# One weight sum per step, and the experts' fifth tile transposed one row tile later

## The chip, the cores and the metric

The kernel runs on one core of a Trainium2 chip. Its time is the device time of one execution in microseconds (us). The engines of the core are named as in the profile: PE is TensorE (PEld its weight load), DVE is VectorE, ACT is ScalarE, POOL is GpSimd, and SP is SyncE, which here does nothing but issue DMA transfers.

## The reference

Three stages follow each other: a linear attention with an exponential feature map, a layer that takes the largest of three products, and a mixture of 8 experts in which each token goes to its two best.

```python
def phi(x):                                   # attention, 4 x 8 heads, 576 tokens, 64 wide
    proj = np.einsum('bhsd,df->bhsf', x, w_phi)
    proj = proj - np.max(np.abs(proj), axis=-1, keepdims=True)
    return np.concatenate([np.exp(proj), np.exp(-proj)], axis=-1)
...
num = np.einsum('bhsf,bhfd->bhsd', q_p, kv)
den = np.einsum('bhsf,bhf->bhs', q_p, z)[..., None] + 1e-06
...
h = np.maximum(np.maximum(x @ w1, x @ w2), x @ w3)      # x: 2304 x 512, w: 512 x 768
x = h @ w_out
...
noisy_logits = x @ w_gate + np.log1p(np.exp(x @ w_noise)) * noise
top2 = np.argpartition(-noisy_logits, 2, axis=1)[:, :2] # softmax over the two gives top2_w
for e in range(8):
    for k in range(2):
        mask = top2[:, k] == e
        h = np.maximum(x[mask] @ w1[e], 0.0)            # w1[e]: 512 x 1024, w2[e]: 1024 x 512
        out[mask] += top2_w[mask, k, None] * (h @ w2[e])
```

## The kernel before

The program is a list of steps, each with a planned time. `at` puts a step at a time, `pe` puts one at the running PE clock and moves that clock on, and `after` puts one at a distance from it. The steps are then issued in the order of their planned times, so a planned time sets only the place in the queue of each engine. PE, ACT, DVE and SP take their instructions in just that order. On POOL a scheduler decides.

Every float32 product is done as three products of shortened numbers: a weight or an activation is split into a high part (an ACT copy) and a low part (a DVE subtraction), as in `split`, and high x high, high x low and low x high are added up in PSUM.

The second stage works on 6 chunks `c` of 384 tokens. For each of 6 column blocks `f` of 128 hidden units it makes three products (`first`, L886, 12 instructions each, `j` = 0, 1, 2), takes their maximum (`larger`: ACT copies the first into a tile `a`, L894, and DVE takes the larger twice, L896), splits it (`hidden`, tiles `hh` and `hl`) and multiplies by the output weights (`second`, L913, 9 instructions), one step later. The product banks `s` are three and are used in turn, so the ACT copy of one step must be done before PE can begin a later one. At the end of a chunk its output goes to memory (`x2_out`), is transposed (L927) and routed; the routing's result is scattered into a table by six indirect DMAs on POOL (L1047). In chunk 0 the last of the weights arrive in 64-bit form and are made narrow on the way: POOL adds two parts (`narrow_add`, L243), DVE masks (L262) and ACT and DVE split them.

The experts 1 to 7 use a seven-product scheme for their first layer, which needs sums and differences of quarters of their weights. These are made during the second stage, 28 of them (7 experts, 4 each). One such sum is: two loads on SP into a buffer `raw` (`quarter_load`), four POOL additions (`quarter_sum`), an ACT copy into the tile `qh`, of which there is one (`quarter_high`), and a DVE subtraction and two stores to the table `sums` on SP (`quarter_out`). There are two buffers with the tag `raw` and one `raw3`; every third sum takes `raw3`. `sum_jobs` plans them: the load 9.5 ahead of the end of a step `f`, the additions 4.5 ahead, the copy and the stores 0.65 behind. One sum stands in each `f` of chunks 1 to 4 but two at `f` = 4 in chunks 1, 2 and 3, and one in chunk 5. In chunk 5 the weights of expert 0 are loaded too (`refill`, `w2_load`).

The experts' part goes over units of up to 608 tokens: 28 `product` steps of 6 instructions each (L1183), then five row tiles of the second layer (`expert2`, L1324, 24 instructions a row tile). Between the row tiles stand the transposes of the next expert's tokens (`turns7`, `turn_x`, L1119), which POOL has gathered (L1109), two tiles ahead; `rows7` then forms the sums and splits of those tokens on ACT and DVE (L1147, L1158, L132). The fifth tile has 96 tokens and is transposed behind row tile 3 (`i == 2`).

Of the kernel before, what the change touches and what calls it, by code (L numbers as in the profile page):

```python
# [9 lines left out]
F32 = mybir.dt.float32  # L10
# [9 lines left out]
P = 128  # L20
# [3 lines left out]
class Plan:  # L24
# [5 lines left out]
    def at(self, t, f, *x):  # L30
        self.ops.append((t, len(self.ops), f, x))
# [7 lines left out]
def tile_linear_attention__then__moe__then__noisy_top2_moe(  # L39
# [28 lines left out]
    F1 = FF1 // P  # L68
# [23 lines left out]
    st, pools = {}, {}  # L92
# [59 lines left out]
    def raw_tile():  # L152
        return stage.tile([P, 1024], F32, name="raw", tag="raw", bufs=2)
# [915 lines left out]
    def sizes(M):  # L1069
        return [min(P, M - i * P) for i in range((M + P - 1) // P)]  # L1070
# [267 lines left out]
    def summed(key, i):  # L1338
        return isinstance(key, int) and key >= SEVEN and i < len(ORDER7) and SEVENTHS[ORDER7[i]][0] == "S"

    def w2_load(key, e, i):
        if summed(key, i):
            return
        raw = raw_tile()
        first_ = len(ORDER7) if isinstance(key, int) and key >= SEVEN else KD
        if i >= first_:
            f = i - first_
            dq.dma_start(raw.rearrange("p (a d) -> p a d", a=2),
                         e_w2[ds(e, 1), f * 2 * P:(f + 1) * 2 * P, :].rearrange("o (a p) d -> p (o a) d", p=P))
        elif first_ == KD:  # L1350
            dq.dma_start(raw, e_w1[ds(e, 1), i * P:(i + 1) * P, :].rearrange("o p f -> p (o f)"))
        else:
            i_, j_ = SEVENTHS[ORDER7[i]][1]
            dq.dma_start(raw.rearrange("p (a f) -> p a f", a=2),
                         e_w1[e, j_ * 2 * P:(j_ + 1) * 2 * P, i_ * (FF2 // 2):(i_ + 1) * (FF2 // 2)]
                         .rearrange("(a p) f -> p a f", p=P))
        st["w2", key, i] = raw
# [148 lines left out]
    def pe(dur, f, *x):  # L1506
        at(clock[0], f, *x)
        clock[0] += dur

    def after(d, f, *x):  # L1510
        at(clock[0] + d, f, *x)

    def first_pe(c, f, j):
        pe(G1, first, c, f, j)
        after(0.05, larger, j)
        if j == 2:
            after(0.6, hidden, c, f)
# [33 lines left out]
    for i, n in enumerate(late_ones[1:]):  # L1551
        t = END + 5.0 + 2.6 * i + 3.0 * (i > 5)
# [7 lines left out]
    def finish(c):  # L1560

        for t in range(CT):
            after(0.05 + 0.5 * t, x2_out, c, t)

    def tail(c, i):
        if i == 0:
            for t in range(2):
                pe(0.45, x2_turn, c, t)
                after(0.0, x2_in, c, t)
            if c < NCHUNK - 1:  # L1570
                after(0.1, begin_route, c)
        elif i == 1:
            pe(0.45, x2_turn, c, 2)
            after(0.0, x2_in, c, 2)
        elif i == 2:
            pe(0.95, gates, c)
            after(0.0, gates_out, c)
        else:
            pe(0.35, gates_turn, c)
            route_at(c, clock[0])  # L1580
# [7 lines left out]
    def base(e):  # L1588
        return 12 + pairs.index((e, 0))
# [10 lines left out]
    def refill(i, n, wait=0.1):  # L1600
        for i in range(i, i + n):
            if i >= len(pairs):
                return
            after(0.0, w2_room, *pairs[i], i + 12)
            if summed(*pairs[i]):
                after(wait + 1.0 + 3.0 * (i % 4), w2_high, *pairs[i])
                continue
            en, j = pairs[i]
            t = max(clock[0] + wait, split_at[-1] + 3.0)
            at(max(split_at[-2] + 0.01, t - 9.0), w2_load, en, en, j)  # L1610
            at(t, w2_high, en, j)
            at(t, w2_low, en, j)
            split_at.append(t)

    def refill_at(i, t, lead):
        if i < len(pairs):
            en, j = pairs[i]
            t += clock[0]
            at(max(split_at[-2] + 1.21, t - lead), w2_load, en, en, j)
            at(t, w2_high, en, j)  # L1620
            at(t + 1.2, w2_low, en, j)
            split_at.append(t)
# [6 lines left out]
    jobs = [(e, a, c) for e in range(SEVEN, E) for a in range(2) for c in range(2)]  # L1629
    todo = list(jobs)  # L1630

    def sum_jobs(n):
        for i, job in enumerate(todo[:n]):
            after(-9.5, quarter_load, *job)
            after(-4.5 + i, quarter_sum, *job)
            after(0.65 + 0.02 * i, quarter_high, *job)
            after(0.66 + 0.02 * i, quarter_out, *job)
        del todo[:n]

    for c in range(NCHUNK):  # L1640
        if c == NCHUNK - 1:
            split_at.append(clock[0] + 25.0)
        for f in range(F1):
            for j in range(3):
                if c or f or j > 1:
                    first_pe(c, f, j)
                if c and j == 2:
                    sum_jobs(2 if f == 4 and c < 4 else 1)
                if c and f == 0 and j == 0:
                    pe(G2, second, c - 1, F1 - 1)  # L1650
                    finish(c - 1)

                tails = TAILS[c == NCHUNK - 1]
                if c and 3 * f + j in tails:
                    tail(c - 1, tails.index(3 * f + j))
            fx = 3 if c else 4
            if f in (fx, fx + 1) and c + 1 < NCHUNK:
                after(0.5, split_x, c + 1, f - fx)
            if c == NCHUNK - 1 and f == F1 - 1:
                break  # L1660
            if f:
                pe(G2, second, c, f - 1)
            if c == NCHUNK - 1 and f % 2 == 1:
                refill(2 * f - 2, 3)
            if c == NCHUNK - 1 and f and f % 2 == 0:
                refill(2 * f - 1, 1)
    c = NCHUNK - 1
# [27 lines left out]
    for n, (e, M, row0) in enumerate(units):  # L1695
# [77 lines left out]
        def turns7(i, n=n):  # L1773
            pe(0.45, turn_x, n + 1, cap, i)
            if i + 2 < len(sizes(cap)):
                after(0.02, gather_x, n + 1, cap, i + 2, N + 1)

        def rows7(j, wait=1.6):
            after(0.5, x_quarters, j)
            after(wait, x_sums, j)  # L1780

        if M <= P:
            pe(0.7 * 2, expert2, n, e, M, 0, range(2))
            pe(0.45, tile_turn, n, 1)
            after(0.0, tile_hidden, n, 1)
            turns7(4)
            rows7(2)
            pe(0.7 * 2, expert2, n, e, M, 0, range(2, 4))
            pe(d2 / 2, expert2, n, e, M, 0, range(4, F2))
            after(0.0, expert_out, n, e, M, 0)  # L1790
        else:
            if nxt and n > 0:
                for i in range(2):
                    turns7(i)
                rows7(0)
            if not nxt:
                after(0.9, settle)
            for i in range(len(sizes(M))):
                if n == 0 and i == 2:
                    pe(0.45, turn_x, 1, cap_b, 0)  # L1800
                    after(0.02, gather_x, 2, cap, 1, N + 1)
                    turns7(0, 1)
                if n == 0 and i == 3:
                    turns7(1, 1)
                    rows7(0)
                pe(d2, expert2, n, e, M, i)
                if n == 0:
                    after((-0.01, -0.01, 0.5, 0.0)[i], expert_out, n, e, M, i)
                else:
                    after(0.95 if nxt and i == 1 else -0.01, expert_out, n, e, M, i)  # L1810
                if n == 0 and i == 2:
                    after(0.51, gather_prev, n, e, M, 3)
                elif n and i + 3 < len(sizes(M)):
                    after(0.96 if nxt and i == 1 else 0.0, gather_prev, n, e, M, i + 3)
                if nxt and n > 1:
                    if i == 1:
                        turns7(2)
                        turns7(3)
                        rows7(1)
                    if i == 2:  # L1820
                        turns7(4)
                        rows7(2)
        if n == 0:
# [3 lines left out]
        if n:  # L1827
            if seven(n):
                i = base(e) + len(ORDER7)
# [3 lines left out]
            else:  # L1833
                i = base(e) + 2
# [61 lines left out]
```

## Time and profile before

| | us |
|---|---|
| median of 3 runs | 947.41 |
| lowest, highest | 946.42, 951.82 |
| profiled execution | 951.02 |
| its span | 949.3 |
| PE busy in the span | 930.8 (98%) |
| PE's weight load busy | 808.1 (85%) |
| DVE, ACT, POOL busy | 609.2, 491.8, 539.4 |

Times within the profile are counted from the start of its span. A row of the timeline is one instruction or a few alike in sequence, with start, duration, engine, line and what it writes and reads; the bracket at its end is the time for which its engine had been idle and what ended that. A matmul's duration overlaps the next one's, so the distance of two starts is what one costs.

### The profile page before, as it was taken

How to read it: one execution, taken by the hardware profiler on the slowest of the kernel's cores; microseconds unless marked ns; L12 is line 12 of the kernel's file. 1: busy time of each engine (PE TensorE's matmuls, PEld its weight loads, DVE VectorE, ACT ScalarE, POOL GpSimd, SP SyncE). 2: the span in 40 equal slices, each digit the busy share in tenths (PEclk: the TensorE clock that was granted, in tenths of full speed). 3: DMA queues.
4: the chain of work that ended last, by engine and by line, in shares of the span. 5: the costliest groups of instructions: out<-in, count | busy, mean ns of one | idle time of the engine just before them, and what ended most of it. 6: DMA issues, size and time to landing. Idle time of an engine off the chain costs nothing. (4 is left out here: it accounts for less than half of the span.)

```text
span 949.3 us, 18471 instructions
## 1 busy us (share of the span) xinstructions
PE 930.8 (98%) x6817; PEld 808.1 (85%) x6817; DVE 609.2 (64%) x1292; ACT 491.8 (52%) x1056; POOL 539.4 (57%) x598
## 2 busy tenths in 40 slices
PE   8999999999999999899999999999999999999997
PEld 7777777889989989799997889798898979799895
DVE  6999998895644546355445357757675767657641
ACT  6999998464333244342335246545363645545340
POOL 6888898454464735456153546555574746546362
PEclk9999999999999999999999999999999999999999
DMA  7666653541567676656446266857575746648312
GB/s 201 174 208 176 187 169 117 197 134 56 187 203 243 181 244 208 196 191 189 157 159 219 68 206 218 292 183 259 168 250 182 279 160 208 238 160 303 96 34 72
DMA packets 129372, 174.91 MB, mean 184 GB/s; under 512 B 35806, under 2 KB 90206, under 8 KB 129282
## 3 DMA queue, kind: packets, MB, share of 16 engines
q1 hardware_dynamic: 117794, 143.79, 47.7%
q0 software_dynamic: 10928, 29.62, 9.3%
q8 instruction: 54, 0.88, 0.4%
q10 hardware_dynamic: 560, 0.33, 0.1%
q14 instruction: 36, 0.29, 0.1%
HBM read 123.05 MB, written 51.24 MB: 184 GB/s over the span
## 5 line engine op out<-in xcount | busy, mean ns | idle before, releaser
L886 PE MATMUL s<-xh,wh 128*128 128x384 f32 x432 | 149.0, 345 | 5.1 <-ACT a L894 4.2
L886 PE MATMUL s<-xh,wl 128*128 128x384 f32 x432 | 146.0, 338 | 0.4 <-DVE wl L278 0.4
L886 PE MATMUL s<-xl,wh 128*128 128x384 f32 x432 | 145.9, 338 | 0.0
L1334 POOL DMA_INDIRECT out_dram<-o,emeta x40 | 49.0, 1224 | 103.0 <-DVE o L1332 51.0
L886 PEld LDWEIGHTS s<-xh,wh 128*128 128x128 f32 x432 | 81.6, 189 | 12.5 <-ACT a L894 5.5
L896 DVE TENSOR_TENSOR a<-s,a 128x384 f32<-128x384 f32 x72 | 39.9, 555 | 72.2 <-PE s L886 71.0
L1324 PE MATMUL p<-wh,hh 128*128 128x512 f32 (+1 forms) x208 | 82.9, 399 | 0.0
L886 PEld LDWEIGHTS s<-xl,wh 128*128 128x128 f32 x432 | 81.7, 189 | 1.4
L1324 PE MATMUL p<-wh,hl 128*128 128x512 f32 (+1 forms) x208 | 82.4, 396 | 0.1
L886 PEld LDWEIGHTS s<-xh,wl 128*128 128x128 f32 x432 | 81.7, 189 | 0.7 <-DVE wl L278 0.7
L1324 PE MATMUL p<-wl,hh 128*128 128x512 f32 (+1 forms) x208 | 82.1, 395 | 0.0
L1409 DVE TENSOR_TENSOR wl<-raw,wh 128x1024 fp32r<-128x1024 f32 x57 | 69.1, 1218 | 14.8 <-ACT wh L1401 14.7
L1183 PE MATMUL s<-gx,wh 128*128 128x304 f32 x336 | 72.5, 302 | 0.0
L1377 POOL TENSOR_TENSOR raw<-raw 128x256 f32<-128x256 f32 x28 | 24.3, 866 | 83.3 <-DMA raw<-in_moe_w_dram 39.8
L1401 ACT ACTIVATE wh<-raw 128x1024 fp32r<-128x1024 f32 x57 | 58.9, 1054 | 24.1 <-PE p L1324 11.2
L1047 POOL DMA_INDIRECT meta<-mt,si x36 | 37.4, 1040 | 48.3 <-DVE si L1043 39.1
L132 DVE TENSOR_TENSOR gx<-t,gx 128x512 fp32r<-128x512 f32 (+3 forms) x88 | 41.0, 481 | 34.3 <-ACT gx L131 34.0
L243 POOL TENSOR_TENSOR nm<-nm,bits 128x512 int32<-128x512 int32 (+1 forms) x32 | 38.2, 1204 | 42.5 <-DVE nm L233 26.6
L1391 DVE TENSOR_TENSOR raw<-raw,qh 128x1024 fp32r<-128x1024 f32 x28 | 37.0, 1320 | 35.6 <-ACT qh L1386 35.6
L131 ACT ACTIVATE hh<-a 128x384 fp32r<-128x384 f32 x36 | 18.8, 522 | 74.4 <-DVE a L896 74.4
L1183 PEld LDWEIGHTS s<-gx,wh 128*128 128x128 f32 x336 | 55.6, 189 | 0.7
L131 ACT ACTIVATE gx<-t 128x512 fp32r<-128x512 f32 (+3 forms) x88 | 36.4, 436 | 38.1 <-DVE t L1158 29.9
(316 smaller groups left out, 2645.4 us busy)
## 6 DMA issues: line engine op xcount, KB each, us to landing
raw<-in_moe_w_dram SPq DMA_DIRECT2D x57, 512.0 KB, 4.5
raw<-in_moe_w_dram SPq DMA_DIRECT2D x56, 256.0 KB, 4.3
sums<-qh SPq DMA_DIRECT2D x28, 512.0 KB, 3.0
sums<-raw SPq DMA_DIRECT2D x28, 512.0 KB, 3.6
wh<-sums SPq DMA_DIRECT2D x28, 512.0 KB, 4.9
wl<-sums SPq DMA_DIRECT2D x28, 512.0 KB, 6.3
bits<-in_moe_w_dram SPq DMA_DIRECT2D x18, 512.0 KB, 5.5
out_dram<-zrow SPq DMA_DIRECT2D x9, 512.0 KB, 4.0
```

The costliest lines, as they stand in the source:

```text
L131: nc.scalar.activation(hi, src, AF.Copy)
L132: nc.vector.tensor_tensor(lo, src, hi.bitcast(F32), op=ALU.subtract)
L243: in_order(nc.gpsimd.tensor_tensor(m_[:, i:i + w], m_[:, i:i + w], low[:, i:i + w], op=ALU.add))
L886: nc.tensor.matmul(p_, a[:, d, fs], b_, start=(n == 0), stop=(n == 3 * KD - 1))
L896: nc.vector.tensor_tensor(a, p_, st.pop("a"), op=ALU.max)
L1047: ins = nc.gpsimd.indirect_dma_start(out=meta, out_offset=bass.IndirectOffsetOnAxis(ap=si[:, t, kk:kk + 1], axis=0), in_=mt[:, t, kk, :], ...
L1183: nc.tensor.matmul(bk["p"], a[:, d, fs], b_[:, d, :], start=(d == 0 and i == 0), stop=(d == 1 and i == 2))
L1324: nc.tensor.matmul(p_, a, b_[:, fw], start=(f == 0 and r == 0), stop=(f == (3 if seven(n) else F2 - 1) and r == 2))
L1334: alone(e, nc.gpsimd.indirect_dma_start(out=out, out_offset=bass.IndirectOffsetOnAxis(ap=mt[:m, i, 1:2], axis=0), in_=o[:m], in_offset=Non ...
L1391: nc.vector.tensor_tensor(lo, t, hi.bitcast(F32), op=ALU.subtract)
L1401: nc.scalar.activation(WE[e, i][0], st["w2", e, i], AF.Copy)
L1409: nc.vector.tensor_tensor(wl, st.pop(("w2", e, i)), wh.bitcast(F32), op=ALU.subtract)
```

## The change

Three things are changed. `sum_jobs` becomes `sum_job`, which plans one sum per call; the loads are planned 15.5 ahead of the step's end and the additions 10.5 ahead. It is called at `j` = 2 of every `f` in chunks 1 to 5 and at the last `f` of chunk 0, so that the first sum falls into chunk 0, and three into chunk 5. At `f` = 3 and 4 the copy and the stores are planned at 1.8 behind the step's end. In the first refill (expert 0) the second, fifth and eighth load take the buffer `raw3`. In the experts the transposes of the fifth tile, and the sums and splits behind them, are planned behind row tile 4 (`i == 3`).

```diff
     def w2_load(key, e, i):
         if summed(key, i):
             return
-        raw = raw_tile()
+        if key == 0 and i % 3 == 1 and "m2" in pools:
+            raw = pools["m2"].tile([P, 1024], F32, name="raw3", tag="raw3")
+        else:
+            raw = raw_tile()
...
-    def sum_jobs(n):
-        for i, job in enumerate(todo[:n]):
-            after(-9.5, quarter_load, *job)
-            after(-4.5 + i, quarter_sum, *job)
-            after(0.65 + 0.02 * i, quarter_high, *job)
-            after(0.66 + 0.02 * i, quarter_out, *job)
-        del todo[:n]
+    def sum_job(t, ahead=15.5):
+        if todo:
+            job = todo.pop(0)
+            after(-ahead, quarter_load, *job)
+            after(5.0 - ahead, quarter_sum, *job)
+            after(t, quarter_high, *job)
+            after(t + 0.01, quarter_out, *job)
...
-                if c and j == 2:
-                    sum_jobs(2 if f == 4 and c < 4 else 1)
+                if j == 2 and (c or f == F1 - 1):
+                    sum_job(1.8 if f in (3, 4) else 0.65)
...
-                    if i == 2:
+                    if i == 3:
                         turns7(4)
                         rows7(2)
```

On ACT, at `f` = 4 of chunk 3 (`a` frees PE's bank, `xh` and `hh` are splits, `qh` is the copy of a weight sum), before:

```order
L894 ACTIVATE a_5345<-s_5315 128x384
L131 ACTIVATE xh<-xT 128x768
L131 ACTIVATE hh<-a_5378 128x384
L1386 ACTIVATE qh<-raw 128x1024 x2
L894 ACTIVATE a_5428<-s_5398 128x384
```

And with the change, at the same place:

```order
L894 ACTIVATE a_5333<-s_5307 128x384
L131 ACTIVATE xh<-xT 128x768
L131 ACTIVATE hh<-a_5363 128x384
L1389 ACTIVATE qh<-raw_5157 128x1024
L894 ACTIVATE a_5407<-s_5378 128x384
```

One copy stands between `hh` and the next `a`, where there were two.

On POOL, in chunk 0 (`nm` are the narrow additions, `raw` the additions of weight sums), before:

```order
L243 TENSOR_TENSOR nm<-nm,bits 128x256 x16
L1377 TENSOR_TENSOR raw<-raw 128x256
L1380 TENSOR_TENSOR raw<-raw 128x256
L1381 TENSOR_TENSOR raw<-raw 128x256
L1382 TENSOR_TENSOR raw<-raw 128x256
```

And with the change:

```order
L243 TENSOR_TENSOR nm<-nm,bits 128x256 x14
L1380 TENSOR_TENSOR raw<-raw 128x256
L1383 TENSOR_TENSOR raw<-raw 128x256
L1384 TENSOR_TENSOR raw<-raw 128x256
L1385 TENSOR_TENSOR raw<-raw 128x256
L243 TENSOR_TENSOR nm<-nm,bits 128x256 x2
```

The first sum's four additions have moved ahead of the last two narrow additions.

On DVE, in the second layer of expert 1 (`o` is the output of a row tile, `gx`, `t` and `b` of width 48 or 96 belong to the next expert's fifth tile), before:

```order
L1409 TENSOR_TENSOR wl<-raw,wh 128x1024
L132 TENSOR_TENSOR gx<-t_7715,gx 128x4x48
L132 TENSOR_TENSOR gx<-t_7715,gx 128x2x48
L1158 TENSOR_TENSOR t_7715<-b_7746,t_7715 128x2x48
L1158 TENSOR_TENSOR t_7715<-t_7715,b_7746 128x2x48
L1158 TENSOR_TENSOR b_7747<-b_7747,t_7715 128x96
L1158 TENSOR_TENSOR t_7715<-t_7715,b_7747 128x2x48
L132 TENSOR_TENSOR gx<-t_7715,gx 128x2x48
L132 TENSOR_TENSOR gx<-b_7747,gx 128x2x48
L132 TENSOR_TENSOR gx<-t_7715,gx 128x4x48
L1332 SCALAR_TENSOR_TENSOR o<-p_7720,emeta,pv 128x512
L1332 SCALAR_TENSOR_TENSOR o<-k,emeta,pv 96x512
```

And with the change:

```order
L1412 TENSOR_TENSOR wl<-raw,wh 128x1024
L1332 SCALAR_TENSOR_TENSOR o<-p_7715,emeta,pv 128x512
L132 TENSOR_TENSOR gx<-t_7748,gx 128x4x48
L132 TENSOR_TENSOR gx<-t_7748,gx 128x2x48
L1158 TENSOR_TENSOR t_7748<-b_7780,t_7748 128x2x48
L1158 TENSOR_TENSOR t_7748<-t_7748,b_7780 128x2x48
L1158 TENSOR_TENSOR b_7781<-b_7781,t_7748 128x96
L1158 TENSOR_TENSOR t_7748<-t_7748,b_7781 128x2x48
L132 TENSOR_TENSOR gx<-t_7748,gx 128x2x48
L132 TENSOR_TENSOR gx<-b_7781,gx 128x2x48
L132 TENSOR_TENSOR gx<-t_7748,gx 128x4x48
L1332 SCALAR_TENSOR_TENSOR o<-k,emeta,pv 96x512
```

The output of row tile 4 now stands ahead of the fifth tile's work. The same holds for experts 2 to 6. On PE the four transposes have moved with it, past 24 products.

## Rows read from the trace of the kernel before

**Rows 1.** Waits of PE: us in total, times, longest.

```profile
PE s L886 <- ACT a L894: 4.2, 3, 3.6
```

**Rows 2.** Windows, five handovers: length, then busy of PE, PEld, DVE, ACT, POOL, PEclk.

```profile
223.13:231.53 8.40, 8.40 (x44) 7.56 (x43) 2.75 (x5) 3.58 (x7) 0.00 (x0) 1.00 0.23 84
276.53:286.52 9.99, 9.07 (x43) 7.35 (x43) 4.43 (x5) 4.97 (x8) 2.48 (x4) 1.00 0.78 260
331.62:341.57 9.95, 9.03 (x43) 7.33 (x43) 4.45 (x5) 4.97 (x8) 2.47 (x4) 1.00 0.78 258
386.58:400.39 13.81, 10.22 (x43) 9.04 (x43) 4.04 (x5) 5.19 (x8) 3.91 (x4) 0.88 0.65 220
445.49:453.90 8.41, 8.41 (x43) 7.57 (x43) 2.34 (x3) 3.76 (x6) 0.10 (x1) 1.00 0.69 218
```

**Rows 3.** Timeline of ACT, third handover: start, duration, what, idle before.

```profile
383.42 1.06 ACT L1386 ACTIVATE qh<-raw 128x1024 fp32r<-128x1024 f32 x1 [3.89 <-POOL raw L1382]
390.94 1.06 ACT L1386 ACTIVATE qh<-raw 128x1024 fp32r<-128x1024 f32 x1 [6.46 <-DMA sums<-qh]
```

**Rows 4.** Windows, after the third handover's wait; PEclk is third from the end.

```profile
392.00:394.00 2.00, 1.57 (x5) 1.57 (x6) 1.87 (x3) 0.37 (x1) 1.77 (x2) 0.66 0.55 181
394.00:396.00 2.00, 2.00 (x8) 2.00 (x8) 0.94 (x2) 0.98 (x2) 0.00 (x0) 0.50 1.00 340
```

**Rows 5.** Timeline of POOL, chunk 0: last narrow pair, last addition of a sum.

```profile
216.09 1.91 POOL L243 TENSOR_TENSOR nm<-nm,bits 128x256 int32<-128x256 int32 x2 [0.78 <-DVE nm L233]
...
221.65 1.07 POOL L1382 TENSOR_TENSOR raw<-raw 128x256 f32<-128x256 f32 x1
```

**Rows 6.** Timeline of SP, chunk 0: the first sum's loads.

```profile
209.75 1.21 SPq L1369 DMA_DIRECT2D raw<-in_moe_w_dram  x2
```

**Rows 7.** Tiles sums, then raw, 225 to 480 us: from issue to landing.

```profile
DMA to landing us min/median/max: 2.9/3.3/9.1
...
DMA to landing us min/median/max: 2.9/4.1/9.1
```

**Rows 8.** Timeline of DVE, end of chunk 0, and chunk 3.

```profile
220.90 1.22 DVE L262 SCALAR_TENSOR_TENSOR nm<-bits,nm 128x512 f32<-128x512 f32 x1
...
224.56 0.95 DVE L132 TENSOR_TENSOR xl<-xT,xh 128x768 fp32r<-128x768 f32 x1
...
378.89 1.50 DVE L132 TENSOR_TENSOR xl<-xT,xh 128x768 fp32r<-128x768 f32 x1
```

**Rows 9.** Timeline of PE: the first product of chunk 1.

```profile
225.22 0.33 PE L886 MATMUL s<-xh,wh 128*128 128x384 f32 x1
```

**Rows 10.** Timeline of POOL, chunk 5: the last gather for expert 0.

```profile
491.87 0.95 POOL L1109 DMA_INDIRECT gx<-x2d,emeta  x1 [0.30 <-issue]
```

**Rows 11.** Timeline of PE, chunk 5: the transposes of its rows.

```profile
501.89 1.02 PE L1119 MATMUL t<-exact,gx 128*128 128x128 f32 x8
```

**Rows 12.** Timeline of ACT, chunk 5: the split behind the first refills.

```profile
483.09 0.53 ACT L131 ACTIVATE hh<-a 128x384 fp32r<-128x384 f32 x1 [2.41 <-DVE a L896]
```

**Rows 13.** Timeline of PE, chunk 5: the products that read it.

```profile
490.56 0.39 PE L913 MATMUL p<-wh,hh 128*128 128x512 f32 x1
```

**Rows 14.** Timeline of PE: fifth tile's transposes in experts 3, 4 and 5.

```profile
718.16 0.49 PE L1119 MATMUL t<-exact,gx 96*128 96x96 f32 x4 [0.17 <-DMA gx<-x2d,emeta]
...
771.85 0.49 PE L1119 MATMUL t<-exact,gx 96*128 96x96 f32 x4 [0.19 <-DMA gx<-x2d,emeta]
...
826.57 0.49 PE L1119 MATMUL t<-exact,gx 96*128 96x96 f32 x4 [1.29 <-DMA gx<-x2d,emeta]
```

**Rows 15.** Timeline of DVE, expert 5: the fifth tile's last split.

```profile
830.89 0.36 DVE L132 TENSOR_TENSOR gx<-t,gx 128x192 fp32r<-128x192 f32 x1 [0.22 <-ACT gx L131]
```

**Rows 16.** Timeline of PE: the first product of expert 6.

```profile
838.14 0.44 PE L1183 MATMUL s<-gx,wh 128*128 128x304 f32 x2
```

**Rows 17.** Timeline of POOL, chunk 3: the last of six scatters.

```profile
377.03 0.96 POOL L1047 DMA_INDIRECT meta<-mt,si  x1 [0.30 <-issue]
```

**Rows 18.** Timeline of SP, chunk 3: the second store of the sum of f = 1.

```profile
356.32 0.37 SPq L1393 DMA_DIRECT2D sums<-raw  x1
```

## The prediction

> **What bounds the kernel now.** I read four views, in this order. The page's busy times say that TensorE is almost never idle, so any gain has to be an idle stretch of TensorE that goes, and the chain that ended last is of no use (it is only the last store). So I went through who waited for whom, for PE alone: the largest entry is the three-way product at L886 waiting for ScalarE's copy `a` [rows 1]. The timeline puts these waits where a chunk hands over to the next one (after f = 5 of a chunk's hidden products). Each handover is the same piece of program (9 products of L913, 12 of L886, 9 of L913, 12 of L886, up to the transposes of L927), so I took the five of them as windows [rows 2]. The reader is to see two lengths: 8.40 and 8.41 us for the first and the last, and 9.99, 9.95 and 13.81 us for the three between. Those three are the handovers after chunks 1, 2 and 3, and these are the chunks in which f = 4 got two weight sums; after chunks 0 and 4 no sum pair stood there.
>
> Why a pair costs time is in ScalarE's timeline before the third handover [rows 3]. `qh` is a tile with one buffer. The first copy into it, at 383.42, had waited 3.89 us for the additions; the second, at 390.94, waited 6.46 us more until the store of the first had landed. Behind it on ScalarE stands the `a` that frees the PSUM bank PE wants. After that stop PE also ran slowly: the granted clock was 0.66 and then 0.50 for the next 4 us, the lower of its two levels, 1.2 GHz instead of 2.4 [rows 4]. The windows of rows 2 hold this cost too.
>
> **The change, part by part.** The sums are made against the profiled execution: 951.02 us, of which 949.3 are the span and 1.7 lie around it; it is 3.6 us above the median of the runs.
>
> *One sum per f.* The number of sums, 28, stays, and so does what each issues: two loads, four additions on GpSimd, one copy, one subtraction, two stores. Gone is the second copy at f = 4 in chunks 1, 2 and 3. With the handover without a pair as the measure, that gives (9.99 - 8.41) + (9.95 - 8.41) + (13.81 - 8.41) = 1.58 + 1.54 + 5.40 = 8.52 us [rows 2]. What is late next there? Each remaining `qh` copy follows the one before it by a whole f step, 36 products of L886 and 9 of L913, and its own additions now start 6 us sooner in the plan; the handovers of 8.40 and 8.41 us show PE without idle when one sum stands there. I take the whole 8.52; the least would be 13.81 - 9.95 = 3.86, if all three stay at the length of the first two. A gain beyond 8.52 has no row to come from.
>
> *The first sum, in chunk 0.* Its four additions now stand on GpSimd ahead of the last two narrow additions (L243). In the trace the narrow pair came at 216.09, with 0.78 us idle before it, and the sum behind it, back to back, until 222.72 [rows 5]. Its load went out at 209.75, in two parts until 210.96 [rows 6], and with a middle landing of 4.1 us [rows 7] it was there at 215.1, when that idle time began. So the same work in the other order ends at 222.72 less 0.78, at 221.94. The narrow pair is then last, so VectorE's L262, which ran at 220.90 [rows 8], starts some 1.0 us later, and with it `xl`, which ended at 225.51. PE began chunk 1's first product at 225.22 [rows 9] and wants that half of `xl` after seven products, some 1.2 us later, at 226.4. 225.51 + 1.04 is 226.55: 0.15 late, 0.3 with a semaphore's time. I take +0.3. Below, 0 (VectorE catches up); above, the further additions that now run beside `xl`: an `xl` beside additions took 1.50 us where this one took 0.95 [rows 8], and the subtraction behind it may grow as much, so +1.1, together +1.4.
>
> The Trainium skill, SBUF — State Buffer, section "SBUF: two separate sides", says that VectorE and GpSimd hold their shared port pair as an exclusive lock for a whole instruction when VectorE reads two tensors in SBUF, so that the other blocks fully. By that rule the 0.95 and 1.50 us are one instruction let through and one that waited, which agrees; it speaks against this edit, and what it would do here is the second rival below.
>
> *The last chunk gets two sums more.* They put a copy (1.06 us) and a subtraction (near 1.23) each on ScalarE and VectorE, the first of them inside the routing chain of chunk 4, whose end GpSimd waits for before it scatters, loads and gathers expert 0's tokens. I price the delay at 2.3 us at most. The last of the four gathers was issued at 491.87 [rows 10] and the transposes that need it ran at 501.89 without a wait [rows 11]: 10.0 us, of which 7.7 are left, and a load or store of this kernel landed after 3.3 or 4.1 us in the middle [rows 7]. Cost 0; with the longest landing, 9.1, it would be 1.4. On SP the last sum's stores now stand between the first and the second refill load, so the second comes later and holds ScalarE's `wh` and the `hh` behind it, which ran at 483.09 [rows 12]; the products that read it started at 490.56 [rows 13], so 7 us cover that.
>
> *Third buffer for the refill.* It lets loads go sooner into a stretch where PE does not wait for them. Nothing either way; the cover is ScalarE's and VectorE's slack just named.
>
> *Fifth tile behind row tile 4.* In experts 1 to 6 the four transposes move past the 24 products of a row tile. In three of them PE stood waiting for the gather: 0.17, 0.19 and 1.29 us, together 1.65 [rows 14]; in the other three it didn't. Now 24 products, near 5.6 us, lie between, so the wait goes whole. Late next are the sums and splits of that tile for the next expert: in the trace the transposes started at 826.57 and the last split ended at 831.25 [rows 15], 4.7 us; the next expert's first product came at 838.14 [rows 16]. With the transposes one row tile later there are some 5.9 us between the two, and the first product needs only the first of the splits. So the cover holds by about 1.2 us for the last split and 4 for the first. I take -1.65; the ends are -2.2 (the weight load behind each wait) and 0 (a new wait of the same size).
>
> Sum: 951.02 - 8.52 - 1.65 + 0.3 = 941.15 us; I forecast 941.0, taking a little of the -2.2. From the median the same end is reached: 951.02 less the 3.84 by which the third handover exceeds the mean of the other two, 9.97, is 947.2, an ordinary run; three pairs at 1.55 and the rest of the sum bring that to 941.2.
>
> **Rivals.** *The waits stay in part* (the change does less than it says). The loads now go out as soon as a buffer's store has landed, beside the next stores, and a later landing lets each of three handovers keep its 1.55 us: 941.0 + 4.65 = 945.7. For it: landings up to 9.1 us [rows 7]. Against it: an f step is longer than most of them, and two handovers with a single sum show nothing.
>
> *Additions that stop VectorE.* At the end of chunk 0 the second sum's additions now run beside VectorE's crunch, and three of its instructions there (the split's subtraction, `xl`, `hl`) each wait out one addition of 1.07 us [rows 5]: PE's wait grows by 3.2 to 3.5 us, which gives 944.2. For it: the `xl` of 1.50 us [rows 8]; against it: that one lost 0.55 us, half as much.
>
> *The third handover's 13.81 is in every run*, and the 3.6 us by which the profiled execution exceeds the median are from elsewhere. Then the sum stands against the median: 947.41 - 10.0 = 937.4. For it: a single profile can't tell; against it: the third handover exceeds its likes by just 3.84.
>
> *GpSimd's queue turns against it* (slower). The sum of f = 4 stood behind the six scatters of L1047 and stands ahead of them now; if its load lands late, the scatters wait, the sum of f = 5 behind them too, and `qh` holds ScalarE and PE at the handover. In chunk 3 the scatters ended at 377.99 [rows 17]. The load can go when the store of f = 1 has landed, which was issued at 356.32 [rows 18]; with the middle landings it is there by 366, before the scatters. With 9.1 us for each it would come at 376, the scatters would end 8 us after its additions, and the next sum would be 4 us late. From there PE idles as it did at 392, at 5.40 us a handover; in all four chunks that is 941.0 + 21.6 = 962.6, in two of them 951.8. It needs two of the longest landings in a row, so it is unlikely.
>
> **How the numbers follow.** The forecast, 941.0, has 0.55, with a range of its own of 938.5 to 942.7. Waits kept in part, 945.7: 0.19. VectorE stopped, 944.2: 0.05. All of it against the median, 937.4: 0.13. GpSimd's queue: 0.08. This kernel's measurement can tell about 0.5% from no change, 4.7 us, so faster is below 942.7 and slower above 952.1. Faster: the forecast and 937.4, less a little for the forecast's upper edge, 0.67; slower, most of the last rival, 0.07; within, 0.26. The range runs from 936.5 to 946.5: it leaves out the last rival, some of the partial one's upper half, and a little below 937.
>
> **What would show it.** The five handovers all near 8.4 us in the windows; `qh` waiting for no store's landing; no stretch in chunks 1 to 4 with a granted clock of 0.5; PE's waits for gathered rows in front of the 96-wide transposes gone; a wait of at most 0.5 us near 226. Wrong would be: PE waits at the handovers with GpSimd's additions as the cause of `qh`, or a new wait of L1183 for `gx` at the head of an expert.

## The result, and the profile after

| | us |
|---|---|
| before, in the comparison | 950.14 median of 8 runs (946.42 to 953.62) |
| after | 940.3 median of 8 runs (939.51 to 941.56) |
| ratio | 0.9898, 95% interval 0.9878 to 0.9918 |
| profiled execution, span | 940.19, 938.6 |
| PE busy in the span | 926.6 (99%) |

The change makes the kernel 1.0% faster; 941.0 us was forecast, in 936.5 to 946.5. The two spans differ by 10.7 us.

The same five handovers as windows, and below them the one behind the last chunk (its first L913 to its first L927), columns as in [rows 2]:

```profile
222.88:232.21 9.33, 8.69 (x44) 7.52 (x43) 4.98 (x7) 5.51 (x9) 2.54 (x3) 1.00 0.40 121
277.21:285.60 8.39, 8.39 (x43) 7.55 (x43) 2.44 (x3) 3.77 (x6) 3.82 (x4) 1.00 0.73 229
330.67:339.08 8.41, 8.41 (x43) 7.57 (x43) 2.34 (x3) 3.77 (x6) 3.54 (x4) 1.00 0.85 261
384.08:392.48 8.40, 8.40 (x44) 7.56 (x44) 2.34 (x3) 3.76 (x6) 2.95 (x4) 1.00 0.76 235
437.54:445.95 8.41, 8.41 (x43) 7.58 (x43) 2.92 (x3) 3.76 (x6) 3.81 (x4) 1.00 0.73 226
491.76:498.69 6.93, 6.62 (x35) 5.11 (x35) 4.75 (x7) 4.96 (x9) 2.49 (x12) 1.00 0.29 106
```

The handovers after chunks 1 to 3 are as long as the undisturbed one, their clock is full, and PE is busy from end to end: 1.60 + 1.54 + 5.41 = 8.55 us gone. The first is 0.93 longer than it was. The last chunk's, in the kernel before:

```profile
499.73:507.01 7.28, 6.84 (x34) 5.18 (x34) 5.56 (x8) 4.91 (x9) 3.55 (x12) 1.00 0.25 91
```

That is 0.35 less. On ScalarE, where the pair of copies ahead of the third handover had waited 3.89 and 6.46 us [rows 3], the two copies that now stand around it, one a step, have no wait in front of them:

```profile
377.80 1.05 ACT L1389 ACTIVATE qh<-raw 128x1024 fp32r<-128x1024 f32 x1
...
385.31 1.04 ACT L1389 ACTIVATE qh<-raw 128x1024 fp32r<-128x1024 f32 x1
```

Among PE's waits (us in total, times, longest) the entry of [rows 1] is gone. The next largest before was that of the transposes:

```profile
PE t L1119 <- DMA gx<-x2d,emeta: 2.4, 4, 1.3
```

With the change it is smaller, and the wait for `xl` is new (at most 0.5 us was forecast). No L1183 waits for `gx`, which was one of the signs of being wrong:

```profile
PE s L886 <- DVE xl L132: 0.6, 1, 0.6
PE t L1119 <- DMA gx<-x2d,emeta: 0.6, 2, 0.4
```

For the experts I cut PE's timeline at the fifth tile's transposes. The pieces between those made in expert 1 and those made in expert 5 (of the rows of experts 2 and 6) are four periods of one expert; before, then after:

```profile
611.29:664.49 53.20, 53.20 (x310) 47.86 (x308) 34.78 (x71) 27.45 (x60) 28.32 (x32) 1.00 0.65 216
664.49:718.16 53.67, 53.51 (x310) 47.80 (x309) 36.50 (x81) 27.42 (x60) 31.46 (x34) 1.00 0.64 216
718.16:771.85 53.69, 53.49 (x308) 47.79 (x309) 37.15 (x80) 27.43 (x60) 30.43 (x34) 1.00 0.64 216
771.85:826.57 54.72, 53.42 (x309) 47.91 (x309) 36.09 (x73) 27.66 (x60) 30.14 (x34) 1.00 0.63 212
```

```profile
608.54:661.81 53.27, 53.27 (x310) 47.88 (x308) 34.77 (x71) 27.34 (x60) 30.62 (x34) 1.00 0.62 218
661.81:715.16 53.35, 53.35 (x311) 47.86 (x310) 36.45 (x80) 27.34 (x60) 31.23 (x34) 1.00 0.62 217
715.16:768.36 53.20, 53.20 (x309) 47.81 (x308) 37.20 (x79) 27.33 (x60) 30.09 (x34) 1.00 0.66 219
768.36:821.57 53.21, 53.21 (x310) 47.81 (x308) 34.92 (x71) 27.65 (x60) 30.85 (x34) 1.00 0.62 210
```

A period without a wait is 53.20 us. The second of the four holds one small product more (of the table that is made in expert 3) and takes 53.33 to 53.35 in every run with the later fifth tile, where nothing waits. So the waits of 0.17, 0.19 and 1.29 us [rows 14] made their periods 0.32, 0.49 and 1.52 longer, 2.33 in all: each cost 0.15 to 0.30 us more than its bracket says. The bracket counts from the end of the matmul before, and matmuls of 0.40 us follow each other at 0.23. From the first L1183 to the last the experts took 347.04 us before (567.66 to 914.70) and take 344.18 (559.86 to 904.04), 2.86 less. Together: 8.55 - 0.93 + 0.35 + 2.86 = 10.83, against 10.7 of span.

### The profile page after: what moved, and what is told of

Same layout as the page of the kernel before. It is cut to its first block, busy times and chain, and to the rows that moved or that the text cites. A ratio compares the mean times of both kernels' runs of the same rounds, so it can differ in the third digit from the quotient of the medians.

```text
span 938.6 us, 18494 instructions
## 1 busy us (share of the span) xinstructions
PE 926.6 (99%) x6817; PEld 806.1 (86%) x6817; DVE 610.9 (65%) x1292; ACT 491.8 (52%) x1056; POOL 539.9 (58%) x598
## 5 line engine op out<-in xcount | busy, mean ns | idle before, releaser
L1183 PE MATMUL s<-gx,wh 128*128 128x304 f32 x336 | 72.5, 302 | 0.0
L1183 PEld LDWEIGHTS s<-gx,wh 128*128 128x128 f32 x336 | 55.6, 189 | 0.7
L1332 DVE SCALAR_TENSOR_TENSOR o<-p,emeta,pv 128x512 f32<-128x512 f32 (+1 forms) x26 | 19.5, 749 | 50.8 <-PE p L1324 42.2
```

What stands on the lines that cost most here:

```text
L1183: nc.tensor.matmul(bk["p"], a[:, d, fs], b_[:, d, :], start=(d == 0 and i == 0), stop=(d == 1 and i == 2))
```

## The experiments

Each was timed in five rounds against the kernel before on the same chip, whose medians in the three groups (the first four, the next four, the last four) were 948.85, 949.15 and 948.97 us. The theory at the start was that of the prediction: the sums spread, one a step, carry the gain, and the third buffer is worth nothing.

**e1_tile: before, with the later fifth tile alone.**

```diff
-                    if i == 2:
+                    if i == 3:
```

> The kernel before with one part of the change alone: the experts' fifth tile transposed behind row tile 4. My theory: only PE's waits for the gathered rows in front of the 96-wide transposes go, 1.65 us in the trace of before and up to 2.2 with the weight load behind each, so the ratio to the kernel before is 0.9977 to 0.9983, about 948.3 us beside 950.1; the three long handovers stay (two near 10 us, one up to 14). Rival (the wait moves to the next expert's first products, because the tile's sums and splits come too late): ratio 1.000 or more and PE waits of L1183 for gx at the head of an expert.

Measured: 946.03 us, ratio 0.9968 (0.9954 to 0.9982). PE's waits at the 96-wide transposes are gone, and the gain, 0.0032 of 949, is 3.0 us where 1.65 was forecast. The experts take 343.99 us. Its third handover, which this edit does not touch, was 11.30 us long, not 13.81:

```profile
386.25:397.55 11.30, 9.04 (x44) 7.32 (x44) 4.04 (x5) 4.94 (x8) 2.69 (x4) 1.00 0.67 223
```

So that length belongs to the single execution, as does the half clock after it; here the granted clock stays at 1.00.

**e2_sums: before, with one sum per f and the longer lead; no third buffer, no later tile.**

```diff
-                if c and j == 2:
-                    sum_jobs(2 if f == 4 and c < 4 else 1)
+                if j == 2 and (c or f == F1 - 1):
+                    sum_job(1.8 if f in (3, 4) else 0.65)
```

> The kernel before with the other part alone: one weight sum per step, loads and additions planned 15.5 and 10.5 ahead, the first sum in chunk 0; no third refill buffer, and the fifth tile where it was. My theory: the handovers after chunks 1, 2 and 3 fall to 8.4 us each (8.5 us gained in all), and the one after chunk 0 grows by 0.9 as in the changed kernel, so about -7.6 us, ratio 0.992, 942.5 us. Rival (the gain is mostly the third buffer or the tile): ratio 0.996 or more.

Measured: 951.38 us, ratio 1.0022 (1.0005 to 1.0038). The theory fell. The handovers after chunks 1 to 3 did become 8.39, 8.41 and 8.39 us, yet the kernel is no faster: the last chunk's handover grew to 13.80 us, and PE stood there before the transposes of expert 0's tokens:

```profile
499.55 0.67 PE L1119 MATMUL t<-exact,gx 128*128 128x128 f32 x4 [3.85 <-DVE gx L132]
```

That row had no wait in the kernel before [rows 11]. Behind the wait the granted clock was at the lower of its two levels, 0.50, and that lengthens this handover too:

```profile
502.00:504.00 2.00, 2.00 (x6) 1.52 (x6) 1.92 (x3) 1.03 (x2) 0.00 (x0) 0.50 0.00 0
```

**e3_spread: the same with the old lead.**

```diff
-    def sum_job(t, ahead=15.5):
+    def sum_job(t, ahead=9.5):
```

> As e2_sums, but the loads and additions keep their old lead of 9.5 and 4.5; only the spreading to one sum per step is left. My theory, that the second copy into the single qh buffer is what held ScalarE and PE: the handovers after chunks 1 to 3 fall to 8.4 us here too, and the one after chunk 0 stays at 8.4, since the first sum's additions no longer stand ahead of the narrow ones; about -8.5 us, ratio 0.991. Rival (the earlier additions are what frees the handovers, because GpSimd's additions behind the scatters are late): at least 1.5 us stay at each of three handovers, -4 us or less, ratio 0.9955 or more, with qh waiting on GpSimd.

Measured: 950.16 us, ratio 1.0013 (0.9997 to 1.003). The five handovers are 8.41, 8.39, 8.41, 8.39 and 8.41. So spreading alone frees them, as my theory said, and the longer lead is what lengthens the first. But the forecast time did not come: the last chunk's handover is 11.72 us, with a wait of 3.05 for the same `gx`.

**e5_pairs_two_qh: before, pairs kept, the second copy of each pair in a tile of its own.**

```diff
-        st["qh", e, a, c] = hi = pools["m1"].tile([P, 4, QC], F32R, name="qh")
+        if jobs.index((e, a, c)) in (5, 12, 19):
+            hi = pools["m2"].tile([P, KD * CW], F32R, name="qh2", tag="x2T", bufs=1)[:, :1024]
+            hi = hi.rearrange("p (k f) -> p k f", k=4)
+        else:
+            hi = pools["m1"].tile([P, 4, QC], F32R, name="qh")
+        st["qh", e, a, c] = hi
```

> The kernel before with its pairs of sums at f = 4 kept, but the second copy of each pair goes into another tile than qh (one that is free at that time), so that it need not wait for the landing of the first one's store. My theory: the copy's wait for the store goes, the handovers after chunks 1 and 2 fall to 8.4 us; the third may keep some, since the load of the sum behind the pair is late for want of a buffer; -3 to -8 us, ratio 0.9915 to 0.997. Rival (it is ScalarE's extra work or the late additions, not the buffer): the handovers keep their 10 us and the ratio is 0.999 to 1.001.

Measured: 943.75 us, ratio 0.9933 (0.9911 to 0.9955), handovers 8.40, 8.39, 8.41, 8.39 and 8.41, last chunk's 7.09. ScalarE, third handover:

```profile
379.81 1.06 ACT L1391 ACTIVATE qh<-raw 128x1024 fp32r<-128x1024 f32 x1 [3.92 <-POOL raw L1382]
381.32 1.06 ACT L1391 ACTIVATE qh<-raw 128x1024 fp32r<-128x1024 f32 x1 [0.45 <-POOL raw L1382]
```

The second copy waits 0.45 us for its additions, not 6.46 for a store. It was the one `qh`, held until its store had landed, that stopped ScalarE and with it PE; that two sums stand in one step costs PE nothing.

What remained open was why spreading costs in the last chunk what it wins in the others, and whether the buffer that I had priced at nothing is what pays for it. e6_no_raw3, e8_raw3_only and e9_pairs_tile are for that, and e7_late_first is for the first handover.

**e6_no_raw3: the changed kernel without the third buffer.**

```diff
-        if key == 0 and i % 3 == 1 and "m2" in pools:
-            raw = pools["m2"].tile([P, 1024], F32, name="raw3", tag="raw3")
-        else:
-            raw = raw_tile()
+        raw = raw_tile()
```

> The changed kernel without the third buffer in the first refill; everything else of the change stays. Theory now (the two sums that the last chunk gains keep both weight buffers, so the refill's loads come late unless there is a third one; the buffer pays for nearly all that was won): it gives back about what the second run (one sum per f step, longer lead, old buffers) lost, so 6 to 8 us over the changed kernel, ratio to before 0.998 to 1.001; the last chunk's handover is 12 to 14 us (6.9 in the changed kernel, 7.3 before), TensorE waits over 2 us there for the transposes L1119 on gx, and ScalarE's wh conversion waits more than 10 us in sum for raw loads. Rival as in the prediction (the buffer is worth nothing either way, and the second run lost its time for want of the later fifth tile): ratio 0.989 to 0.992, handover about 7 us.

Measured: 946.4 us, ratio 0.997 (0.9957 to 0.9983); the changed kernel had 0.9898. It gives back 6 to 7 us; the ratio is a little under the forecast one. The last handover, and the steps that lead to it, on SP, ScalarE, VectorE and PE:

```profile
492.45:505.00 12.55, 8.24 (x35) 6.32 (x34) 7.55 (x10) 7.37 (x12) 3.52 (x12) 0.86 0.40 119
```

```profile
473.01 3.39 SPq L1351 DMA_DIRECT2D raw<-in_moe_w_dram  x2
...
478.23 1.06 ACT L1401 ACTIVATE wh<-raw 128x1024 fp32r<-128x1024 f32 x1 [6.53 <-DMA raw<-in_moe_w_dram]
...
495.59 1.06 ACT L1401 ACTIVATE wh<-raw 128x1024 fp32r<-128x1024 f32 x1 [2.04 <-DMA raw<-in_moe_w_dram]
...
496.55 1.07 ACT L131 ACTIVATE gx<-t 128x512 fp32r<-128x512 f32 x2
496.68 1.23 DVE L1409 TENSOR_TENSOR wl<-raw,wh 128x1024 fp32r<-128x1024 f32 x1 [1.78 <-ACT wh L1401]
497.82 0.68 DVE L132 TENSOR_TENSOR gx<-t,gx 128x512 fp32r<-128x512 f32 x1
...
498.56 0.53 PE L1119 MATMUL t<-exact,gx 128*128 128x128 f32 x4 [3.78 <-DVE gx L132]
```

And in the changed kernel:

```profile
469.82 4.07 SPq L1354 DMA_DIRECT2D raw<-in_moe_w_dram  x3
...
475.18 1.06 ACT L1404 ACTIVATE wh<-raw 128x1024 fp32r<-128x1024 f32 x1 [3.42 <-DMA raw<-in_moe_w_dram]
...
492.25 0.69 DVE L132 TENSOR_TENSOR gx<-t,gx 128x512 fp32r<-128x512 f32 x1 [1.25 <-ACT gx L131]
```

Read it downward. The last sum's second store was issued at 469.35 in this kernel. With two buffers the refill's second load needs that sum's buffer and goes 3.7 us later; with a third it goes 0.4 us after the store that stands before it (469.41). The later loads are late too, since each takes a buffer that a split gives back: ScalarE waits 12.7 us in 5 waits for raw loads, against 3.4 in one. The last `wh` but one then stands on ScalarE, and its `wl` on VectorE, in front of the two halves of `gx`, which PE is waiting for. The waiting weights are not what PE needs; they stand in the queues of the engines that it needs.

The wait is not all of it. The handover is 5.62 us longer than in the changed kernel, and the brackets of its two waits (3.78 and 0.53) make 4.31. Behind them the granted clock was at the lower of its two levels:

```profile
500.00:502.00 2.00, 2.00 (x7) 1.62 (x7) 1.61 (x3) 1.63 (x4) 0.00 (x0) 0.50 0.00 0
```

The products of L913 follow each other there at 0.43 us instead of 0.23.

**e8_raw3_only: before, with the third buffer alone** (the lines above, added).

> The kernel before with the third buffer in the first refill as the only edit. Theory (the buffer pays only where two more sums stand in the last chunk): ratio 0.999 to 1.001, last chunk's handover 7.0 to 7.3 us as before, the five handovers as before (8.4, 10, 10, 11 to 14, 8.4). Rival (the buffer is a gain by itself, and the change's gain comes from it): ratio 0.992 to 0.995 with the handovers as before and less time in the expert stage.

Measured: 949.66 us, ratio 1.0004 (0.9987 to 1.002); the last handover is 6.94 us where it was 7.28, the third 10.67. By itself the buffer is worth nothing that can be measured. It is worth 6 us only where two sums more stand in the last chunk.

**e7_late_first: the changed kernel, the first sum's additions planned later.**

```diff
-            after(5.0 - ahead, quarter_sum, *job)
+            after(-4.5 if job == jobs[0] else 5.0 - ahead, quarter_sum, *job)
```

> The changed kernel, but the additions of the first weight sum (the one in chunk 0) are planned at -4.5 instead of -10.5, behind the last narrow pair; its load, conversion and store stay. Theory (the additions at 215 to 220 us hold GpSimd's last narrow pair back, VectorE waits 1.3 us for it and TensorE 0.65 us for xl): the handover after chunk 0 is 8.4 us again (9.33 in the changed kernel) with no TensorE wait for xl, 0.9 us less, ratio to before 0.988 to 0.989. Rival (the handover is long because the conversion and the store of this sum lie in it): stays at 9.2 to 9.4 us, ratio 0.990. A second rival: the later additions make the store land behind the next sum's conversion and the next handover grows by a few us, ratio 0.992 to 0.995.

Measured: 939.18 us, ratio 0.9892 (0.987 to 0.9914). The first handover is 8.40 us, so its 0.93 did come from the place of the additions:

```profile
224.69:233.09 8.40, 8.40 (x43) 7.57 (x43) 5.01 (x6) 4.57 (x8) 3.57 (x4) 1.00 0.47 143
```

In time it can't be told from the changed kernel.

**e9_pairs_tile: e5_pairs_two_qh with the later fifth tile.**

> The kernel before with two edits: the second sum of each pair is copied into a tile of its own, so that no copy waits for a store, and the fifth tile goes behind row tile 4; the pairs, their times and the refill's buffers stay. Theory (the handovers after chunks 1 to 3 and the expert stage's waits add up; no extra sums come to the last chunk and none to chunk 0): ratio 0.9933 times 0.9968 = 0.990, handovers all 8.4 us, last chunk's about 7.1, as fast as the changed kernel. Rival (the two edits share a part of their gain): 0.992 to 0.993.

Measured: 939.72 us, ratio 0.9902 (0.988 to 0.9924), all five handovers 8.39 to 8.41, the last chunk's 7.13. The pairs by themselves were not the fault: with a second place for the copy they cost as little as the spread sums, and nothing in the last chunk has to be paid for.

**e10_sums_raw3: the changed kernel with the fifth tile back behind row tile 3.**

```diff
-                    if i == 3:
+                    if i == 2:
```

> The changed kernel with the fifth tile back behind row tile 3, so the sums and the third buffer alone. Theory (the buffer pays for the last chunk's two extra sums, and the later fifth tile is an independent 3 us): ratio 0.993 (0.9915 to 0.9945), the five handovers 9.3, 8.4, 8.4, 8.4, 8.4, the last chunk's about 7.0, and TensorE waits of 1.5 to 4.5 us in sum at the 96-wide transposes. Rival (the tile's gain and the buffer's overlap): ratio 0.990 as the whole change, or 0.996 and above if the buffer alone does not bring the last chunk back.

Measured: 943.94 us, ratio 0.9948 (0.9928 to 0.9968), a little above the band; the last handover is 6.93. The same two edits that one by one gave 1.0022 and 1.0004 give 0.9948 together. In its profile PE waits 2.7 us for the tiles of L1119, 2.2 of them at the 96-wide transposes, and not for gathers alone:

```profile
PE t L1119 <- DVE o L1332: 1.7, 2, 0.9
PE t L1119 <- DMA gx<-x2d,emeta: 1.0, 3, 0.5
```

**e11_after_again, e12_late_first_again, e13_pairs_tile_again: the changed kernel, e7_late_first and e9_pairs_tile once more, side by side.**

> The changed kernel once more, on the same chip and beside the next two, so that they can be set against it: ratio 0.990, five handovers 9.3, 8.4, 8.4, 8.4, 8.4.

> The changed kernel with the first sum's additions behind the last narrow pair, once more. Theory: first handover 8.4 again, 0.9 us under the changed kernel of this chip, ratio to before 0.989. Rival (what it wins at the handover is lost in the phase ahead of chunk 0): equal to the changed kernel within 0.3 us.

> The pairs with a tile of their own for the second copy and the later fifth tile, once more. Theory (all handovers at 8.4 and no sum in chunk 0): 0.5 to 1 us under the changed kernel of this chip, ratio 0.989 to 0.990. Rival: equal to it within 0.3 us.

Measured: 939.63 (ratio 0.9895, 0.9873 to 0.9917), 939.54 (0.9891, 0.9869 to 0.9913) and 938.94 us (0.9891, 0.9868 to 0.9915). The three are equal within what can be measured; no version is shown to beat the changed kernel, and the 0.9 us forecast for the second one did not come. Its first handover is 8.40 us again. Both profiles of that version reach this handover some 1.8 us later than the changed kernel's do (224.69 and 224.59 against 222.88 and 222.81). The moved additions are not the cause: GpSimd's narrow pair at 200 us, some 15 us ahead of the first addition that moves, is already 1.7 us late; it starts at 201.35 and 201.28 where the changed kernel's profiles have 199.65 and 199.49. What the cause is stays open.

## Why the prediction was right, point by point

*One sum per f, 8.52 us.* Right to 0.03 us in the profile, and with the mechanism named (e5_pairs_two_qh). But a part of it was the luck of one execution: other profiles with pairs show 11.30 and 10.67 us at the third handover; by these the edit is worth 6.0 and 5.4 us. The third rival, that 13.81 stands in every run, is refuted by the same two profiles.

*The first sum, +0.3 us (0 to 1.4).* The mechanism was right, the size was 0.93. On GpSimd and VectorE in the changed kernel:

```profile
219.87 1.89 POOL L243 TENSOR_TENSOR nm<-nm,bits 128x256 int32<-128x256 int32 x2
...
223.68 0.74 POOL L1384 TENSOR_TENSOR raw<-raw 128x256 f32<-128x256 f32 x1
```

```profile
221.79 1.22 DVE L262 SCALAR_TENSOR_TENSOR nm<-bits,nm 128x512 f32<-128x512 f32 x1 [1.33 <-POOL nm L243]
223.71 1.26 DVE L278 TENSOR_TENSOR wl<-nm,wh 128x512 fp32r<-128x512 f32 x1 [0.70 <-ACT wh L276]
...
226.02 0.95 DVE L132 TENSOR_TENSOR xl<-xT,xh 128x768 fp32r<-128x768 f32 x1
```

The narrow pair ends at 221.76 (221.94 was forecast) and L262 starts 0.89 us later than in [rows 8] (1.0 forecast). But PE reached this handover 0.25 us sooner (222.88, not 223.13), so beside PE it is 1.14 later. What I had left to the second rival is `wl`. Before, it ran alone and took 0.69 us:

```profile
222.82 0.69 DVE L278 TENSOR_TENSOR wl<-nm,wh 128x512 fp32r<-128x512 f32 x1 [0.70 <-ACT wh L276]
```

Now it starts 0.03 us after an addition of the second sum and takes 1.26: 0.57 more, where 0.71 of the addition were left. 1.14 and 0.57 are the 1.71 by which, beside PE, `xl` ends later, where the forecast had 1.04. `xl` itself runs after the last addition and takes the 0.95 of [rows 8]. So of the three instructions in the second rival one waited, and for less than the rest of one addition. The `xl` of 1.50 us in [rows 8] is the same case: 0.05 us before it an addition of 0.74 us had begun, of which 0.69 were left, and it took 0.55 more. On GpSimd, before:

```profile
378.84 0.74 POOL L1380 TENSOR_TENSOR raw<-raw 128x256 f32<-128x256 f32 x1
```

The Trainium skill (SBUF — State Buffer, "SBUF: two separate sides") states an exclusive lock between the two engines, held for a whole instruction, when VectorE reads two tensors in SBUF. `wl` reads two, and the trace agrees in the main: with a full block to the end of the addition it would have taken 1.40 us, not 1.26.

The +0.3 also held 0.15 for a semaphore, for which I had no row. Here PE's product starts 0.05 us after the end of `xl`, and the next one follows at 0.28 where 0.17 is usual: 0.16 together, though no row shows a semaphore by itself.

*The last chunk, "cost 0", and the third buffer, "nothing either way".* This is the step that failed. Their sum was right, -0.35 us for 0; the two parts are about +6 and -6 (e6_no_raw3 beside the changed kernel; e2_sums beside e10_sums_raw3 gives 7). That two errors cancelled was luck. The path that I did follow, the gathers, held: in none of these profiles does PE wait for a gather there. I also said that the second refill load would come later and that 7 us between `hh` and its products cover it. I did not follow it to the loads behind it, of which each takes the buffer that the one before gives back, nor to ScalarE and VectorE, where the last splits stand ahead of `gx`, nor to the clock, which stood at 0.50 behind the wait. I priced the buffer in the kernel before, where it is worth nothing, and not in the program that the other edits make.

*Fifth tile, -1.65 us (-2.2 to 0).* The mechanism was right, the size too small: -2.86 in the profile, 3.0 in e1_tile, and 943.94 - 939.63 = 4.3 between e10_sums_raw3 and e11_after_again. There are four reasons. The waits cost more than their brackets: the three of [rows 14] took 2.33 us, just beyond the end that I had set. Next, 0.55 of the 2.86 is a wait of transposes that this edit does not move, those of a third tile in expert 1, before and after:

```profile
604.61 0.51 PE L1119 MATMUL t<-exact,gx 128*128 128x128 f32 x4 [0.72 <-DMA gx<-x2d,emeta]
```

```profile
596.22 0.51 PE L1119 MATMUL t<-exact,gx 128*128 128x128 f32 x4 [0.17 <-DMA gx<-x2d,emeta]
```

Third, the waits differ from run to run: without the edit the experts took 347.04, 349.73, 347.71, 349.03, 348.22 and 347.93 us in six profiles, and the one shown was the lowest; with it eight profiles lie between 343.86 and 344.63. Fourth, I priced the gathers alone; without the edit PE waits there for VectorE's `o` as well (e10_sums_raw3). Its periods from expert 2 to expert 5, where the changed kernel has 53.35, 53.20 and 53.21:

```profile
655.89:709.79 53.90, 53.58 (x310) 47.96 (x310) 36.65 (x81) 27.42 (x60) 31.11 (x34) 1.00 0.64 215
709.79:763.44 53.65, 53.49 (x308) 47.80 (x309) 36.95 (x80) 27.45 (x60) 29.99 (x34) 1.00 0.63 216
763.44:817.78 54.34, 53.53 (x309) 47.85 (x309) 35.59 (x73) 27.66 (x60) 30.46 (x34) 1.00 0.62 213
```

*The other rivals.* Waits kept in part: no, no handover keeps any. GpSimd's queue turned against it: no, the four handovers behind its scatters are at 8.4 us.

*The base.* The sum was made against 951.02 us of one execution and gave 941.15; the changed kernel's profiled execution took 940.19. Against the three runs shown, 947.41, I expected 6.4 us less, and the ratio says 9.7 (950.14 in eight runs, 949 in the later ones). The profiled execution lay 0.9 to 2.2 us above these medians and the three runs 1.4 to 2.7 below them. Over many runs the handovers gave less than the profile had shown and the experts more, and that the time was hit so closely rests on both.

## What to carry to other kernels

Where work is moved to another place, follow the buffers that it holds there, and the queue behind each instruction that then comes late, as far as PE; price an added buffer in the new program, not in the old one. Where a copy waits for a store, try a second tile before a new order, if there is room: it gave the same time here with none of the side costs. Size a wait by the length of the piece of program around it, with the same piece where nothing waits beside it, and in more than one execution.

## What I had not expected

The changed kernel is also steadier: its runs lie within 2.05 us (939.51 to 941.56), those before within 7.2 (946.42 to 953.62). What went were waits for landings, and in the profiles these vary: 10.67 to 13.81 us at one handover, 2.7 us at the experts. That they are all of the difference was not shown.
